# Block-sparse attention and a bilinear FFN on one core: weights loaded after a piece of keys, values scaled per head pair, a third gather place

## The chip, the cores and the metric

One core of a Trainium2 chip runs the whole program. The metric is the device time of one execution in microseconds (us). TensorE (PE, with its weight loads PEld), VectorE (DVE), ScalarE (ACT), GpSimd (POOL) and SyncE (SP) each work through a queue of their own in order; SP, ACT and POOL also issue DMAs.

## The reference

Four batches, eight heads, 768 tokens, head width 64, in blocks of 32 tokens (24 blocks a batch). A query block sees its neighbour blocks, the first, the last and three sampled blocks; the first and last query blocks see all keys.

```python
scores = scale * np.matmul(q, k.transpose(0, 1, 3, 2))
...
scores = np.where(mask, scores, -1000000000.0)
scores = scores - np.max(scores, axis=-1, keepdims=True)
attn = np.exp(scores)
attn = attn / (np.sum(attn, axis=-1, keepdims=True) + 1e-09)
x = np.matmul(attn, v)          # 3072 tokens x 512
out = (x @ w_a) * (x @ w_b) @ w_out   # d_ff 1536
```

The FFN weights come as 64-bit floats; queries, keys and values as 32-bit floats.

## The kernel before

**Units.** A unit is one query block of one batch with its eight heads; 96 units, batch after batch, in chunks of eight (256 tokens). `attend` is a sparse unit, `attend_all` and `attend_quad` the first and last block of a batch. Batch 0 is computed in plain 32-bit floats. Batches 1 to 3 split each scaled operand into a high and a low 16-bit part. When a chunk's eight units are done, `first_products` (L1429) and `second_products` (L1512 to L1514) run its FFN; these matmuls are most of PE's work.

**Order.** No queue is ordered on the chip. `Plan` is a list scheduler that runs while the program is built: each step is a generator that yields what it needs (an `Event`, a place of a `Ring`, or an engine with an estimated time), and the plan emits the step that can begin first, with a rank to break ties. The emitted order is fixed, and each engine's queue then waits in order on the chip. Every estimated time, rank and ring size thus shapes the order of all queues.

**Weights.** `weights(n)` loads 36 pieces of 512 KB (w_a, w_b, w_out of 12 slices) on POOL's queue (L898), the first two right at the start, into six raw places: three fill `stage`, three fill `keysT[1]`. `convert` turns each into 32-bit floats with three DVE operations (L919, L922, L925), bounds it on ACT (L939), and splits it (L946, L947). `weight_scale` sets the scales and multiplies three factors into `f1` in two operations (L958, L961). `stage_freed` fires when the last weights have left `stage`.

**Start.** `keys(0, g)` issues four pieces of batch 0's keys on ACT's queue (L540), `plain_values_in` three pieces of its values there (L590), `plain_queries` its queries on SP's (L878).

**Keys and values of batches 1 to 3.** `keys` and `values` load four head pairs each (`raw_tile`: a ring of `RAW_BUFS = 4` quarters of `stage`). Keys get a scale for each pair. Values: each pair is bounded (L618), then `values_scale` waits for all four bounds, sets one scale for the batch (`set_scale`: an all-reduce on POOL, L440, and three small DVE operations, L443, L446, L449), and only then each pair is split (L629, L630) and stored to the DRAM tensor `vd` on SP's queue (L635).

**Values for a unit.** `gather_after` (SP's queue, L769 to L783) fetches a unit's value blocks into one of `VG_BUFS = 2` places `VG`; a place comes free when the matmuls of the unit two before (`values_into`, L1043) have read it. The starts of the sampled blocks are read into SP's registers for up to four units at a time (L666).

**In a unit.** Scores to PSUM (L975 in batch 0, L984 later), the row maximum (DVE, L1135), its scaling (DVE, L1139 in batch 0, L1141 later), the exponentials (ACT, L1147), the split (L1003, L1006, L1010), a DMA transpose on SP's queue into one of `PT_BUFS = 3` places `pt` (L1187), the values (L1043), and `output`, which divides by the sums (L1348 to L1356).

Of the kernel before, what the change touches and what calls it, by code (L numbers as in the profile page):

```python
# [10 lines left out]
F16 = mybir.dt.float16  # L11
# [36 lines left out]
SM_BUFS = 3  # L48
LATE = 16
AT_ONCE = 4  # L50
NEAR = 8
# [243 lines left out]
def kernel(  # L295
# [55 lines left out]

    stage = kvp.tile([P, RAW_BUFS, 2 * NT * D], F32, name="stage")
    keysT = [kvp.tile([P, H, S], F16, name=f"keysT{i}") for i in range(2)]
    vd = [dram.tile([S, ROW], F16, name=f"vd{b}") for b in range(B)]
# [14 lines left out]
    at_g = at_w + 3 * NF  # L369
    n_at = at_g + NC  # L370
    bound = const.tile([P, n_at], F32, name="bound")
    bound_v = const.tile([P, B * NG], F32, name="bound_v")
    power = const.tile([P, n_at], F32, name="power")
# [14 lines left out]
    eye = const.tile([P, P], F32, name="eye")  # L388
    mark = const.tile([1, 1], F32, name="mark")
    offs = const.tile([1, NB, NR], I32, name="offs")  # L390
    offs_k = const.tile([1, NB, NR], I32, name="offs_k")
# [135 lines left out]
    def raw_tile(b, g, n):  # L527

        yield stage_freed
        t = stage[:, raw_taken[0] % RAW_BUFS]  # L530
        raw_taken[0] += 1
        freed = yield from take("raw", RAW_BUFS)
        return t, freed

    raw_taken = [0]

    def keys(b, g):
        if b == 0:
            t = yield load_way(
                1000, lambda: nc.scalar.dma_start(plain_keys[:, g], k[0, g]), 100000  # L540
            )
            k_ready[0].fire(t)
            return
# [64 lines left out]
    def values(b, g):  # L608

        yield from gate(order[b, 0] - GATE_KV)  # L610
        raw, freed = yield from raw_tile(b, g, 1)
        yield pool_load(1000, lambda: nc.gpsimd.dma_start(raw, v[b, g]))
        if g + 1 < NG:
            plan.start(values(b, g + 1), order[b, 0] - LEAD_V)
        elif b + 1 < B:
            plan.start(keys(b if b == 1 else b + 1, 0), order[b, 0] - LEAD_K)
        t = raw.rearrange("p (t x) -> p t x", t=NT)
        end = yield act(1020, lambda: nc.scalar.activation(  # L618
            junk.rearrange("p f c -> p (f c)")[:, : NT * P].rearrange("p (t x) -> p t x", t=NT),
            t, AF.Abs, accum_out=bound_v[:, b * NG + g : b * NG + g + 1],  # L620
        ))
        v_bound[b].fire(end)
        if g == NG - 1:
            plan.start(values_scale(b), order[b, 0] - LEAD_V)
        yield v_scale[b]
        done = yield from take("ks", KS_BUFS)
        vs = work.tile([P, NT, 2, 2 * D], F16, tag="ks", name=f"vs{b}_{g}", bufs=KS_BUFS)
        s = scale[:, at_v + b : at_v + b + 1]
        yield act(930, lambda: nc.scalar.activation(vs[:, :, 0], t, AF.Copy, scale=s))  # L629
        end = yield dve(1015, lambda: nc.vector.scalar_tensor_tensor(  # L630
            vs[:, :, 1], t, s, vs[:, :, 0], ALU.mult, ALU.subtract
        ))
        freed.fire(end)
        yield SPARE
        end = yield sp(650, 1350, lambda: nc.sync.dma_start(  # L635
            vd[b][:, g * 4 * D : (g + 1) * 4 * D].rearrange("(t p) x -> p t x", p=P),
            vs.rearrange("p t a x -> p t (a x)"),
        ))
        done.fire(end)
        v_stored[b].fire(end)  # L640

    def values_scale(b):
        yield v_bound[b]
        at = at_v + b
        yield dve(150, lambda: nc.vector.reduce_max(
            bound[:, at : at + 1], bound_v[:, b * NG : b * NG + (NG if b else NT // 2)],
            axis=mybir.AxisListType.X,
        ))
        end = yield from set_scale(slice(at, at + 1))
        v_scale[b].fire(end)  # L650
# [31 lines left out]
    def gather_keys(n):  # L682
# [39 lines left out]
        k_free[b].fire(t)  # L722

    def plain_vg(n):
        t = VG[n % VG_BUFS].rearrange("p a x -> p (a x)").bitcast(F32)
        return t.rearrange("p (a x) -> p a x", a=2)
# [27 lines left out]
    def gather_after(n):  # L754
        b, i, x = vg_units[n]
        vg_free[n] = yield from take("vg", VG_BUFS)
        if n + 1 < len(vg_units):
            plan.start(gather_values(n + 1), order[vg_units[n + 1][:2]] - LEAD_G)
        to, of, row = VG[n % VG_BUFS], vd[b], ROW
        if b == 0:  # L760
            to, of, row = plain_vg(n), plain_values, H * D
        dense = i in (0, NB - 1)
        first = vg_holds.get(n % VG_BUFS) != b
        vg_holds[n % VG_BUFS] = None if dense else b

# [118 lines left out]
    def weights(n):  # L884

        f, i = divmod(n, 3)
        if n == 0:
            yield from gate(W_GATE)
        at = n % W_BUFS if n < W_EARLY else W_BUFS // 2 + n % (W_BUFS // 2)
# [210 lines left out]
    def attend(b, i):  # L1100
# [82 lines left out]
        mine = yield from turn("pt", b, i)  # L1183
        kept = yield from take("pt", PT_BUFS)
        mine.fire(0)
        pt = work.tile([P, 8, P], F16, tag="pt", name=f"pt{n}", bufs=PT_BUFS)
        t = yield sp(1300, 1500, lambda: nc.sync.dma_start_transpose(  # L1187
# [5 lines left out]
        yield from before(b, i)  # L1193
        vg = VG[m % VG_BUFS]
        quads = [
# [23 lines left out]
    def attend_quad(b, i, hq, ends):  # L1219
# [52 lines left out]
        for x in range(2):  # L1272
# [13 lines left out]
            freed[x].fire(t)  # L1286
            kept = yield from take("pt", PT_BUFS)
            if x == 1:
                mine_pt.fire(0)
            pt = work.tile([P, 6, P], F16, tag="pt", name=f"pt{n}_{hq}{x}", bufs=PT_BUFS)  # L1290
            t = yield sp(1100, 1130, lambda hl=hl, pt=pt: nc.sync.dma_start_transpose(
# [5 lines left out]
    def all_values(b, i, hq, x, pt, kept):  # L1297
# [17 lines left out]
        else:  # L1315
            vg = VG[m % VG_BUFS].rearrange("p a x -> p (a x)")
            terms = [
# [10 lines left out]

    ride = [Event() for _ in units]
    quad_sent = {(b, i): Event() for b in range(B) for i in (0, NB - 1)}  # L1330
    all_done = {
# [3 lines left out]
    def output(b, i, bank, read):  # L1335
# [288 lines left out]
```

## Time and profile before

| | |
|---|---|
| three timed runs | 803.25, 807.28, 808.39 us, median 807.28 |
| the profiled execution's own time, its span | 803.08 us, 801.3 us |
| busy: PE, DVE, ACT, POOL | 742.4, 533.6, 490.9, 227.6 us |
| mean granted TensorE clock | 0.983 of full speed |
| DMA | 131.8 MB, 164 GB/s over the span |
| the chain of waits by engine | PE 65%, DVE 13%, DMA 9%, issue 5%, ACT 4%, SP's queue 3% |

PE's busy time counts pipelined matmuls whose ends are modelled. The chain of waits is followed back from the last instruction, at each step to what released it. A wait for several semaphores is put down to the one that came last.

### The profile page before, as it was taken

The numbers are of one execution on the slowest core, as the hardware profiler recorded it, in microseconds if no ns is written. First come the engines' busy times: TensorE is split into PE (matmuls) and PEld (weight loads), VectorE is DVE, ScalarE is ACT, GpSimd is POOL, SyncE is SP. The second block draws the span as 40 slices with busy tenths as digits, with TensorE's granted clock in tenths as the row PEclk, the third lists the DMA queues.
The fourth block names the chain that finished last, engine by engine and source line by source line (L and its number), as shares of the span: only waits on it lengthen the run. The fifth ranks groups of instructions, "written<-read, shape, count | busy, mean of one in ns | idle before, by whom it ended". The sixth has DMA issues, their size and how long they took to land.

```text
span 801.3 us, 25888 instructions
## 1 busy us (share of the span) xinstructions
PE 742.4 (93%) x10056; PEld 522.5 (65%) x10056; DVE 533.6 (67%) x1504; ACT 490.9 (61%) x1202; POOL 227.6 (28%) x532
## 2 busy tenths in 40 slices
PE   2759789899998989999999999999989999999997
PEld 0426568674567748757758758658658757768853
DVE  5899999975666677676577686667667775322132
ACT  2666888786656677776466686565566664333333
POOL 5535833212233432202233432302234320000001
PEclk9879999999999999999999999999999999999999
DMA  8776786865577899897579998968687788310001
GB/s 270 234 215 196 228 249 189 266 131 135 126 186 163 182 197 226 179 231 155 144 180 170 214 239 170 210 172 171 155 179 164 147 158 167 91 34 1 2 1 53
DMA packets 184135, 131.80 MB, mean 164 GB/s; under 512 B 135627, under 2 KB 155724, under 8 KB 184012
## 3 DMA queue, kind: packets, MB, share of 16 engines
q1 hardware_dynamic: 170860, 82.89, 50.3%
q0 software_dynamic: 11616, 44.05, 17.5%
q10 hardware_dynamic: 1536, 3.21, 1.3%
q8 instruction: 79, 1.29, 0.7%
q14 instruction: 44, 0.36, 0.2%
HBM read 87.63 MB, written 11.01 MB: 123 GB/s over the span
## 4 chain that ended last, share of the span: by engine, by line
PE 65%; DVE 13%; DMA 9%; issue 5%; ACT 4%; SPq 3%; POOL 0%; POOLq 0%; ACTq 0%; DVEq 0%
PE ab L1429 37%; PE o L1512 6%; PE o L1514 5%; PE o L1513 5%; PE av L1043 5%; PE s L984 4%; DMA VG<-vd 4%; DMA vd<-vs 2%; DMA vp<-in_v_dram 2%; DVE low L1135 1%; SPq L666 1%; DVE wab L947 1%; SPq L783 1%; PE s L1120 1%; PE s L975 1%
## 5 line engine op out<-in xcount | busy, mean ns | idle before, releaser
L1429 PE MATMUL ab<-xT,wab 128*128 128x256 f16 x3456 | 393.2, 273 | 2.8 <-DVE g L1448 2.1
L1429 PEld LDWEIGHTS <-wab 128*128 128x128 f16 x3456 | 332.8, 98 | 58.1 <-issue 16.9
L1448 DVE TENSOR_TENSOR g<-g,ab 128x256 f32<-128x256 f32 x144 | 60.4, 419 | 112.9 <-ACT g L1445 109.3
L1445 ACT ACTIVATE g<-ab,f 128x256 f32<-128x256 f32 x144 | 67.7, 470 | 104.2 <-PE ab L1429 103.2
L1483 DVE SCALAR_TENSOR_TENSOR gh<-g,scale,gh 128x256 f16<-128x256 f32 x144 | 69.5, 494 | 72.0 <-ACT gh L1482 70.9
L1482 ACT ACTIVATE gh<-g,scale 128x256 f16<-128x256 f32 x144 | 70.7, 504 | 74.5 <-PE o L1514 70.6
L1512 PE MATMUL o<-wo,gh 128*128 128x512 f16 x288 | 110.1, 382 | 0.0
L1513 PE MATMUL o<-wo,gh 128*128 128x512 f16 x288 | 109.5, 380 | 0.0
L1514 PE MATMUL o<-wo,gh 128*128 128x512 f16 x288 | 109.5, 380 | 0.0
L710 POOL COPY KG<-keysT 128x128 int32 (+1 forms) x264 | 89.0, 375 | 44.6 <-POOL KG L701 22.5
L701 POOL COPY KG<-keysT 128x384 int32<-128x384 int32 (+1 forms) x86 | 50.6, 589 | 164.6 <-PE s L984 146.0
L1147 ACT ACTIVATE sm<-s,low,cq 128x256 f32<-128x256 f32 x132 | 73.6, 559 | 31.7 <-DVE low L1141 15.6
L440 POOL PARTITION_ALL_REDUCE power<-bound x58 | 25.8, 447 | 180.1 <-DVE bound L1462 103.7
L1043 PE MATMUL av<-VG,pt 128*32 128x128 f16 (+2 forms) x3488 | 63.5, 212 | 13.0 <-DMA VG<-vd 9.4
L1010 DVE SCALAR_TENSOR_TENSOR hl<-sm,hl 128x256 f16<-128x256 f32 (+1 forms) x156 | 69.8, 453 | 1.8 <-ACT hl L1003 0.5
L1135 DVE TENSOR_REDUCE low<-s 128x2 f32<-128x512 f32 x88 | 60.1, 683 | 14.9 <-PE s L984 12.0
L1043 PEld LDWEIGHTS <-pt 128*32 128x32 f16 x2688 | 33.1, 97 | 35.4 <-issue 26.6
L1512 PEld LDWEIGHTS <-gh 128*128 128x128 f16 x288 | 28.2, 98 | 36.9 <-issue 6.0
L1514 PEld LDWEIGHTS <-gh 128*128 128x128 f16 x288 | 28.2, 98 | 34.3 <-issue 0.5
L1513 PEld LDWEIGHTS <-gh 128*128 128x128 f16 x288 | 28.3, 98 | 29.1 <-issue 0.3
L1452 ACT ACTIVATE junk<-g 128x1024 f16<-128x1024 f32 x36 | 38.0, 1055 | 10.4 <-DVE g L1448 10.2
L1006 DVE TENSOR_SCALAR hl<-sm 128x256 f16<-128x256 f32 (+1 forms) x113 | 36.3, 325 | 11.7 <-DMA pt<-hl 8.9
(136 smaller groups left out, 932.3 us busy)
## 6 DMA issues: line engine op xcount, KB each, us to landing
VG<-vd SPq DMA_DIRECT2D x210, 64.0 KB, 3.0
VG<-vd SPq DMA_DIRECT2D x66, 192.0 KB, 3.7
q<-in_q_dram POOLq DMA_DIRECT2D x18, 512.0 KB, 4.9
VG<-vd SPq DMA_DIRECT2D x24, 384.0 KB, 3.7
out_dram<-ou POOLq DMA_DIRECT2D x24, 256.0 KB, 3.6
stage<-in_v_dram POOLq DMA_DIRECT2D x12, 384.0 KB, 4.5
vd<-vs SPq DMA_DIRECT2D x12, 384.0 KB
stage<-in_k_dram POOLq DMA_DIRECT2D x12, 384.0 KB, 6.5
```

The costliest lines, as they stand in the source:

```text
L710: nc.gpsimd.tensor_copy(to[:, :, (5 + r) * w : (6 + r) * w], of[:, :, bass.ds(at, w)])
L1010: t = yield dve(221 + n * 1.03, lambda: nc.vector.scalar_tensor_tensor(lo, sm, over, hi, ALU.mult, ALU.subtract))
L1043: mm(both[hs, :, i % 2, hq] if two else av[hs, i % 2, hq], pt[:, y, hs], of if two or b == 0 else of[:, 0], start=(i % 2 == 0 and hq == 0 ...
L1135: yield dve(685, lambda: nc.vector.tensor_reduce(mx, ps, axis=mybir.AxisListType.X, op=ALU.max, negate=True))
L1147: t = yield act(750, lambda hq=hq: nc.scalar.activation(sm[:, hq], ps[:, hq], AF.Exp, bias=low[:, at, hq, 0:1], scale=factor_of(b, cc, hq) ...
L1429: mm(ab[:, i, :].rearrange("p (j x q) -> p j x q", j=PER // 2, x=2), wab[:, f, i, part, kt, :], xc[:, :, a, :, kt, :], start=(i == 0 and k ...
L1445: yield act(460, lambda: nc.scalar.activation(g, ab[:, 0, :], AF.Copy, scale=f1[:, f : f + 1]))
L1482: yield act(400, lambda: nc.scalar.activation(gh[:, 0], g, AF.Copy, scale=s))
L1483: t = yield dve(480, lambda: nc.vector.scalar_tensor_tensor(gh[:, 1], g, s, gh[:, 0], ALU.mult, ALU.subtract))
L1512: mm(po, gh[:, 0, js], wo[:, f, 0], start=(f == 0), stop=False)
L1513: mm(po, gh[:, 0, js], wo[:, f, 1], start=False, stop=False)
L1514: mm(po, gh[:, 1, js], wo[:, f, 0], start=False, stop=(f == NF - 1))
```

## The change

- The weights' loads start when the second piece of batch 0's keys has landed (`k_early`); a copy of one key element on POOL makes POOL's queue wait for it.
- The scaling of the maxima in batch 0 moves from DVE to ACT.
- `f1` takes one DVE operation in place of two.
- Each head pair of values in batches 1 to 3 gets its own scale, right after its bound. `values_even` then takes the largest of the four, and the ratio of each to it enters the divisor in `output`, with the factor that was there.
- `stage` keeps two raw places for keys and values in place of four. The other half becomes, once the weights have left it, a third gather place for batches 1 to 3 and a fourth place for transposed probabilities.

```diff
+    spare = stage.rearrange("p g x -> p (g x)")[:, RAW_PLACES * 2 * NT * D :]
 def raw_tile(b, g, n):
         yield stage_freed
-        t = stage[:, raw_taken[0] % RAW_BUFS]
+        t = stage[:, raw_taken[0] % RAW_PLACES]
         raw_taken[0] += 1
-        freed = yield from take("raw", RAW_BUFS)
+        freed = yield from take("raw", RAW_PLACES)
 def keys(b, g):
+            if g == 1:
+                k_early.fire(t)
             k_ready[0].fire(t)
 def values(b, g):
-            t, AF.Abs, accum_out=bound_v[:, b * NG + g : b * NG + g + 1],
-        ))
+            t, AF.Abs, accum_out=bound[:, at : at + 1],
+        ))
+        end = yield from set_scale(slice(at, at + 1))
         v_bound[b].fire(end)
         if g == NG - 1:
-            plan.start(values_scale(b), order[b, 0] - LEAD_V)
-        yield v_scale[b]
+            plan.start(values_even(b), order[b, 0] - LEAD_V)
-        s = scale[:, at_v + b : at_v + b + 1]
+        s = scale[:, at : at + 1]
+    def values_even(b):
+        yield v_bound[b]
+        at, to = at_p + (b - 1) * NG, at_v + b
+        yield dve(150, lambda: nc.vector.reduce_max(
+            rscale[:, to : to + 1], rscale[:, at : at + NG], axis=mybir.AxisListType.X
+        ))
+        def factors():
+            for x in range(2):
+                ps = slice(x * D, (x + 1) * D)
+                nc.vector.tensor_scalar(
+                    evened[ps, b], scale[ps, at : at + NG].rearrange("p (a i) -> p a i", i=2)[:, :, x],
+                    rscale[ps, to : to + 1], float(2.0 ** 14), ALU.mult, ALU.mult,
+                )
+        end = yield dve(320, factors)
+        v_scale[b].fire(end)
+    def split_vg(m):
+        at = vg_at[m]
+        if at < VG_BUFS:
+            return VG[at]
+        return spare[:, :ROW].bitcast(F16).rearrange("p (a x) -> p a x", a=2)
+    vg_at = [m % VG_BUFS if m < n_plain else (m - n_plain) % 3 for m in range(len(vg_units))]
+    def take_vg(m):
+        at = vg_at[m]
+        if at >= VG_BUFS:
+            yield stage_freed
+        ev = Event()
+        last = vg_user.get(at)
+        vg_user[at] = ev
+        if last is not None:
+            yield last
+        return ev
 def gather_after(n):
-        vg_free[n] = yield from take("vg", VG_BUFS)
+        vg_free[n] = yield from take_vg(n)
 def weights(n):
         if n == 0:
-            yield from gate(W_GATE)
+            yield k_early
+            yield pool(120, lambda: nc.gpsimd.tensor_copy(mark_w, plain_keys[0:1, 1, 0:1]))
 def weight_scale(f):
-        end = yield dve(160, lambda: nc.vector.tensor_mul(
-            f1[:, f : f + 1], rscale[:, at : at + 1], rscale[:, at + 2 : at + 3]
-        ))
-        end = yield dve(160, lambda: nc.vector.tensor_mul(
-            f1[:, f : f + 1], f1[:, f : f + 1], rscale[:, at + 1 : at + 2]
+        end = yield dve(165, lambda: nc.vector.scalar_tensor_tensor(
+            f1[:, f : f + 1], rscale[:, at : at + 1], rscale[:, at + 1 : at + 2],
+            rscale[:, at + 2 : at + 3], ALU.mult, ALU.mult,
         ))
 def attend(b, i):
         if b == 0:
-            yield dve(165, lambda: nc.vector.tensor_scalar(mx, mx, D ** -0.5, None, ALU.mult))
+            yield act(200, lambda: nc.scalar.mul(mx, mx, D ** -0.5))
...
-        kept = yield from take("pt", PT_BUFS)
+        pt, kept = yield from place_pt(f"{n}", 8)
...
-        vg = VG[m % VG_BUFS]
+        vg = split_vg(m)
+    def place_pt(name, cols):
+        freed = yield from take("pt_split", PT_BUFS + 1)
+        at = pt_taken[0] % (PT_BUFS + 1)
+        pt_taken[0] += 1
+        if at == PT_BUFS:
+            yield stage_freed
+            t = spare[:, ROW : ROW + 4 * P].bitcast(F16).rearrange("p (a x) -> p a x", x=P)
+            return t[:, :cols], freed
+        return work.tile([P, cols, P], F16, tag="pt", name=f"pt{name}", bufs=PT_BUFS), freed
 def output(b, i, bank, read):
-            yield dve(165, lambda: nc.vector.tensor_scalar(
-                dn, dn, EPS, float(2.0 ** 14), ALU.add, ALU.mult
+            yield v_scale[b]
+            yield dve(165, lambda: nc.vector.scalar_tensor_tensor(
+                dn, dn, EPS, evened[:, b].unsqueeze(1).to_broadcast([P, 2, HQ]),
+                ALU.add, ALU.mult,
             ))
```

## Rows read from the trace of the kernel before

**Rows 1.** Stages: window, length, then busy us (count) per engine, clock, DMA, GB/s.
```profile
0.00:12.50 12.50, 0.35 (x4) 0.21 (x4) 3.51 (x22) 1.49 (x2) 3.27 (x8) 1.00 0.86 241
12.50:28.00 15.50, 10.98 (x116) 4.71 (x116) 14.56 (x29) 7.72 (x22) 12.26 (x28) 1.00 0.97 308
28.00:61.00 33.00, 20.24 (x352) 11.67 (x352) 30.08 (x87) 22.52 (x61) 13.76 (x30) 0.73 0.69 208
61.00:125.00 64.00, 55.83 (x906) 39.37 (x908) 62.77 (x157) 50.91 (x138) 37.52 (x73) 0.95 0.74 218
125.00:300.00 175.00, 164.00 (x2246) 112.98 (x2239) 128.77 (x366) 121.40 (x294) 54.65 (x131) 1.00 0.73 175
300.00:700.00 400.00, 394.79 (x5752) 285.78 (x5750) 268.50 (x781) 251.68 (x619) 102.19 (x256) 1.00 0.83 177
700.00:801.30 101.30, 96.16 (x695) 67.76 (x693) 25.44 (x66) 35.22 (x70) 3.98 (x8) 1.00 0.05 18
```

**Rows 2.** PE's waits, 0 to 125 us: total us, times, longest.
```profile
PE av L1380 <- DVE xs L1356: 14.9, 6, 5.2
PE s L1120 <- DVE mrows L516: 8.3, 1, 8.3
PE s L975 <- POOL KG L710: 4.9, 1, 4.9
```

**Rows 3.** PE's waits, 125 to 700 us.
```profile
PE av L1043 <- DMA VG<-vd: 9.4, 8, 2.4
```

**Rows 4.** Timeline of the first 28 us: start, duration, engine, line, idle before.
```profile
2.64 0.68 POOL L898 DMA_DIRECT2D stage<-in_moe_w_a_dram  x1
12.53 0.36 DVE L701 COPY KG<-keysT 128x384 f32<-128x384 f32 x1 [4.27 <-DMA keysT<-in_k_dram]
26.83 1.06 ACT L600 ACTIVATE va<-vp 128x1024 f16<-128x1024 f32 x1 [3.38 <-DMA vp<-in_v_dram]
```

**Rows 5.** DMA queues, 0 to 6 us: packets, MB, share (q10 is ACT's).
```profile
q10 hardware_dynamic: 428, 1.17, 59.5%
```

**Rows 6.** DMA queues, 6 to 10 us (q1 is SP's, q0 POOL's).
```profile
q10 hardware_dynamic: 128, 0.37, 40.4%
q1 hardware_dynamic: 104, 0.35, 37.7%
q0 software_dynamic: 62, 0.25, 26.1%
```

**Rows 7.** Chain of waits, pieces between 75 and 100 us: start, us, what.
```profile
80.32 0.08 DVE low L1139
92.36 0.12 DVE power L443
```

**Rows 8.** Instructions by line: count, ns min/median/max, first and last start.
```profile
L1139 DVE TENSOR_SCALAR low<-low x22: 149/162/1273, 17.7 to 150.4; 128x2 f32<-128x2 f32 x22
L1147 ACT ACTIVATION_READ_ACCUMULATOR sm<-s,low x44: 189/198/218, 18.9 to 153.5; 128x1 f32 x44
L961 DVE TENSOR_TENSOR f<-f,rscale x12: 125/149/239, 44.3 to 164.6; 128x1 f32<-128x1 f32 x12
L440 POOL PARTITION_ALL_REDUCE power<-bound x58: 307/356/1192, 28.3 to 769.5; - x58
```

**Rows 9.** Chain of waits, two pieces between 238 and 245 us.
```profile
238.56 2.50 SPq L666
242.99 2.40 DMA VG<-vd
```

**Rows 10.** SP's queue: its waits, 125 to 700 us.
```profile
SPq L778 <- PE av L1043: 27.7, 19, 6.5
```

**Rows 11.** Timeline: key and value pieces of batch 2, first loads to last stores.
```profile
275.93 1.10 POOL L546 DMA_DIRECT2D stage<-in_k_dram  x2
297.37 1.02 DVE L564 SCALAR_TENSOR_TENSOR ks<-stage,scale,ks 128x768 f16<-128x768 f32 x1
351.91 1.80 SPq L635 DMA_DIRECT2D vd<-vs  x2
```

More of the change, by code (lines that the diff above doesn't have):

```diff
@@ L49 @@
 LATE = 16
+RAW_PLACES = 2
 AT_ONCE = 4
@@ L369 @@
     at_g = at_w + 3 * NF
-    n_at = at_g + NC
+    at_p = at_g + NC
+    n_at = at_p + (B - 1) * NG
     bound = const.tile([P, n_at], F32, name="bound")
-    bound_v = const.tile([P, B * NG], F32, name="bound_v")
+    bound_v = const.tile([P, NT // 2], F32, name="bound_v")
+    evened = const.tile([P, B, HQ], F32, name="evened")
     power = const.tile([P, n_at], F32, name="power")
@@ L389 @@
     mark = const.tile([1, 1], F32, name="mark")
+    mark_w = const.tile([1, 1], F32, name="mark_w")
     offs = const.tile([1, NB, NR], I32, name="offs")
@@ L529, in raw_tile @@
         yield stage_freed
-        t = stage[:, raw_taken[0] % RAW_BUFS]
+        t = stage[:, raw_taken[0] % RAW_PLACES]
         raw_taken[0] += 1
-        freed = yield from take("raw", RAW_BUFS)
+        freed = yield from take("raw", RAW_PLACES)
         return t, freed
     raw_taken = [0]
+    k_early = Event()
     def keys(b, g):
@@ L617, in values @@
         t = raw.rearrange("p (t x) -> p t x", t=NT)
+        at = at_p + (b - 1) * NG + g
         end = yield act(1020, lambda: nc.scalar.activation(
             junk.rearrange("p f c -> p (f c)")[:, : NT * P].rearrange("p (t x) -> p t x", t=NT),
-            t, AF.Abs, accum_out=bound_v[:, b * NG + g : b * NG + g + 1],
+            t, AF.Abs, accum_out=bound[:, at : at + 1],
         ))
+        end = yield from set_scale(slice(at, at + 1))
         v_bound[b].fire(end)
         if g == NG - 1:
-            plan.start(values_scale(b), order[b, 0] - LEAD_V)
-        yield v_scale[b]
+            plan.start(values_even(b), order[b, 0] - LEAD_V)
         done = yield from take("ks", KS_BUFS)
         vs = work.tile([P, NT, 2, 2 * D], F16, tag="ks", name=f"vs{b}_{g}", bufs=KS_BUFS)
-        s = scale[:, at_v + b : at_v + b + 1]
+        s = scale[:, at : at + 1]
         yield act(930, lambda: nc.scalar.activation(vs[:, :, 0], t, AF.Copy, scale=s))
@@ L645, in values_scale @@
         yield dve(150, lambda: nc.vector.reduce_max(
-            bound[:, at : at + 1], bound_v[:, b * NG : b * NG + (NG if b else NT // 2)],
+            bound[:, at : at + 1], bound_v,
             axis=mybir.AxisListType.X,
@@ L722, in gather_keys @@
         k_free[b].fire(t)
+    def split_vg(m):
[3 more added lines that the diff above has]
+        return spare[:, :ROW].bitcast(F16).rearrange("p (a x) -> p a x", a=2)
+    n_plain = sum(u[0] == 0 for u in vg_units)
+    vg_at = [m % VG_BUFS if m < n_plain else (m - n_plain) % 3 for m in range(len(vg_units))]
+    vg_user = {}
+    def take_vg(m):
[8 more added lines that the diff above has]
+        return ev
     def plain_vg(n):
@@ L755, in gather_after @@
         b, i, x = vg_units[n]
-        vg_free[n] = yield from take("vg", VG_BUFS)
+        vg_free[n] = yield from take_vg(n)
         if n + 1 < len(vg_units):
             plan.start(gather_values(n + 1), order[vg_units[n + 1][:2]] - LEAD_G)
-        to, of, row = VG[n % VG_BUFS], vd[b], ROW
         if b == 0:
             to, of, row = plain_vg(n), plain_values, H * D
+        else:
+            to, of, row = split_vg(n), vd[b], ROW
         dense = i in (0, NB - 1)
-        first = vg_holds.get(n % VG_BUFS) != b
-        vg_holds[n % VG_BUFS] = None if dense else b
+        first = vg_holds.get(vg_at[n]) != b
+        vg_holds[vg_at[n]] = None if dense else b
         def copies():
@@ L1183, in attend @@
         mine = yield from turn("pt", b, i)
-        kept = yield from take("pt", PT_BUFS)
+        pt, kept = yield from place_pt(f"{n}", 8)
         mine.fire(0)
-        pt = work.tile([P, 8, P], F16, tag="pt", name=f"pt{n}", bufs=PT_BUFS)
         t = yield sp(1300, 1500, lambda: nc.sync.dma_start_transpose(
@@ L1286, in attend_quad @@
             freed[x].fire(t)
-            kept = yield from take("pt", PT_BUFS)
+            pt, kept = yield from place_pt(f"{n}_{hq}{x}", 6)
             if x == 1:
                 mine_pt.fire(0)
-            pt = work.tile([P, 6, P], F16, tag="pt", name=f"pt{n}_{hq}{x}", bufs=PT_BUFS)
             t = yield sp(1100, 1130, lambda hl=hl, pt=pt: nc.sync.dma_start_transpose(
@@ L1315, in all_values @@
         else:
-            vg = VG[m % VG_BUFS].rearrange("p a x -> p (a x)")
+            vg = split_vg(m).rearrange("p a x -> p (a x)")
             terms = [
@@ L1329 @@
     ride = [Event() for _ in units]
+    pt_taken = [0]
+    def place_pt(name, cols):
[7 more added lines that the diff above has]
+        return work.tile([P, cols, P], F16, tag="pt", name=f"pt{name}", bufs=PT_BUFS), freed
     quad_sent = {(b, i): Event() for b in range(B) for i in (0, NB - 1)}
```

## The prediction

> **What bounds the kernel now.** I read the busy times by stage first [rows 1]. TensorE is busy 394.8 of 400 us from 300 to 700, and 164.0 of 175 from 125 to 300: there it is the bound. Before 125 us it is not: busy 0.35 + 10.98 + 20.24 + 55.83 = 87.4 of 125 us, so 37.6 us idle. After 125 us its idle time is 11.0 + 5.2 + 5.1 = 21.3 us, of which the last 5.1 are the final stores. So a change can gain time only by shortening the 37.6 us, or the 16.2 us between 125 and 700.
>
> Next I read who TensorE waits for. Up to 125 us [rows 2]: 8.3 us for the mask tables, 4.9 us for the first gathered keys, and 14.9 us for the divided sums from VectorE. VectorE itself is busy 30.08 + 62.77 = 92.9 of the 97 us from 28 to 125 [rows 1]; it is the bound of that stretch, and what it is spared there ends the stretch earlier. From 125 to 700 one wait stands out [rows 3]: 9.4 us in 8 places for gathered values. The DMA queues and the SP queue then say why each is late.
>
> **The change, part by part.**
>
> *Weights behind keys.* Batch 0's keys are 8 x 768 x 64 x 4 bytes = 1.57 MB. By 6 us ACT's DMA queue has sent 1.17 MB [rows 5]; of the 0.40 MB left it sends 0.37 in the next 4 us, sharing with queries and the first weights [rows 6]. So the keys are out at about 10.3 us, and VectorE sees them at 12.53 [rows 4]. Without the weights' queue the 0.97 MB of rows 6 are shared by two queues: 0.49 MB each in 4 us, so 0.40 takes 3.3 us, to 9.3: 1.0 us gained. From above it is 4.2 us, since the mask is ready only at 8.3 us [rows 2]. From below it is a loss: half of the keys are out by about 4.7 us (estimate from 1.17 MB at 6 us, the flow beginning near 2.5), seen 2.2 us later as above, so the first weights are issued near 7 in place of 2.64 us [rows 4], a slip of 4.4 us that VectorE pays in full if it has nothing else to do. I take -1.0, near what the queue shares give: VectorE is busy 14.56 of 15.5 us after 12.5 [rows 1], with key copies, maxima and value copies to fill with. Behind the waiting copy POOL's queue holds only weights and key gathers, and the latter need the keys anyhow.
>
> Beside this a rule: the Trainium skill, "DMA: Bandwidth & Descriptors", section "Issuing engines are not separate DMA queues", says that DMAs of all issuing engines run on the same 16 engines and interleave. The trace agrees: three queues share 0.97 MB in 4 us with none idle [rows 6]. By that rule the weights lose what the keys gain; this term would be 0 and the sum -8.0.
>
> *Maxima on ScalarE.* 22 operations leave VectorE [rows 8]. Each lasts 0.162 us, but overlaps the one before it, and the chain shows 0.08 [rows 7]: 22 x 0.08 = -1.8 us, between 0 (if it filled gaps) and -3.6 (full length). What ScalarE pays for a two-element operation no row shows; the nearest is its one-element read of an accumulator, 0.198 us [rows 8]: 0 to 22 x 0.198 = 4.4 us. ScalarE idles 97 - 73.4 = 23.6 us from 28 to 125 [rows 1], which hides it; without that cover it is +4.4.
>
> *One f1 operation less.* 12 of 0.149 us [rows 8], net 0.08: -1.0 us, to -1.8 at full length.
>
> *Scales per head pair.* Twelve all-reduces in place of three, and three small VectorE operations with each. A small one costs 0.08 to 0.12 us [rows 7], so 9 x 3 x 0.1 = 2.7 us for three batches, 0.9 for batch 1; `values_even` has three small operations a batch in place of one maximum, +0.2. Only batch 1 falls in VectorE's stretch or just behind it: +1.1. For batches 2 and 3 VectorE is 67% busy (268.5 of 400 us) [rows 1], which hides it; without that cover +2.2 more. POOL pays 9 x 0.356 = 3.2 us [rows 8]; it is busy 102 of 400 us. Each new all-reduce waits on POOL for its bound from ScalarE, with key gathers queued behind; they are a unit ahead.
>
> *Third gather place.* A gather must wait until the values of the unit two before are used. SP waits for that 27.7 us in 19 places [rows 10], then loses up to 2.50 us to a register load, and the DMA takes 2.40 us [rows 9]; TensorE pays 9.4 us. With three places the gather may go one unit sooner, some 7 us (96 units in about 700 us): more than the register load and the landing together. But SP still issues in one order, and the transposes stand between. I take two thirds, -6.3, between 0 and -9.4. What is late next is the transposes, and ScalarE and VectorE in front of them.
>
> *Fourth transposed place, two raw places.* I cost them at nothing. The first only loosens a ring. The second is hidden by the FFN's stock: after 700 us TensorE still has 96.2 us of work [rows 1], so attention may slip some without TensorE running dry. Without this cover it is the last rival.
>
> Sum: -1.0 - 1.8 - 1.0 + 1.1 - 6.3 = **-9.0 us**. Against the profiled execution's 803.08 us that is 794.1. The four executions shown (803.08, 803.25, 807.28, 808.39) have the middle 805.3, 2.2 above the profiled one, and the timed median is 4.2 above it. I add 2.2: **796 us**.
>
> **The rivals.** A difference under 1% (8.1 us of 807.28) is about what a measurement of this kernel cannot tell from none: under 799.2 is faster, over 815.4 slower.
>
> - *SP's order is the limit, not the place.* The gather gets its place earlier but goes out where the planner puts it, behind transposes and register loads [rows 9]. For it: the 2.50 us register load is not touched. Against: the 27.7 us wait for a place [rows 10]. Then only the start's -2.7 stays: 805.3 - 2.7 = 802.6. Chance 18%.
> - *Values first.* With the weights behind, all three pieces of batch 0's values may be issued at once; the last is seen at 26.83 us now [rows 4], though half of the loads before it were weights. TensorE idles 4.5 us from 12.5 to 28 and 12.8 from 28 to 61 [rows 1]; if a third of these 17.3 us goes, that is -5.8 more: 790. Against: the values' issue waits its turn on ScalarE's queue. Chance 10%.
> - *A new fixed order with new stalls.* Every changed estimate re-orders all queues; a gain of 9.0 us is of the size of the present eight stalls [rows 3]. The places and scales then do what they say, but as much is lost elsewhere: 803 to 808. That the change does not do what it says belongs here: the keys' landing may be early enough already that the wait shifts nothing. Chance 13%.
> - *Slower: two raw places.* A pair of pieces holds its place from the load to the split, 297.37 + 1.02 - 275.93 = 22.5 us [rows 11]. Eight pieces through two places take 4 x 22.5 = 90 us; now the last stores of batch 2 are issued by 353.7, after 77.8 us [rows 11]. So the values of a batch come 12 us later. It decides only if TensorE has no FFN work ready for those 12 us; after 125 us it nearly always has, which speaks against. If two batches go uncovered: 805.3 - 9.0 + 24 = 820. Chance 9%.
>
> **How the numbers follow.** My forecast has 50%, with a range of its own of 788 to 802: the start terms between +1 and -6, the gather term between -3 and -9.4, and 2 for the spread of executions. Of this I put 44 points under 799.2. Faster: 44 + 10 + 4 (the low end of the first rival) = 58%. Within 1%: 6 + 14 + 13 = 33%. Slower: 9%. The range, 785 to 808, takes in the three milder rivals and leaves out the last one and the far ends.
>
> **What would show it.** Keys: the first score matmul at about 12.5 in place of 13.6 us, and the first weights' load issued near 7 us. Maxima and f1: VectorE's busy time down by some 4 us in the first 150 us, ScalarE's up by 2 to 4. Gather: TensorE's wait for gathered values after 125 us falls from 9.4 to about 3 us, SP's wait for a place to a third. Idle before 125 us falls from 37.6 to about 35. My forecast is wrong if the values' wait stays near 9 us, if the maxima's stretch is bound by ScalarE, or if TensorE shows waits for keys or stored values where a batch begins.

## The result, and the profile after

The changed kernel's median is 813.29 us (805.98 to 818.79, 22 executions), that of the kernel before beside it 808.54 (803.00 to 813.51, 22). The ratio is 1.0059 [1.0034, 1.0083]: slower by some 4.8 us, where 796 with a range of 785 to 808 was forecast. Ratios in this text leave out executions that ran over 1.5% above the fastest of their kernel (six of the twelve of e2); medians and ranges do not.

The first profile of the changed kernel was taken in an execution of 818.79 us, the longest of the 22. A second one (e9 below) was of 808.85 us, span 807.1. It stands near the low end of its range, and the 803.08 us of the kernel before at the low end of theirs, so I compare these two and use the first profile only where it shows a wait more plainly. Two profiles of one order can differ: the first one idles 33.3 us before 125 us, like the second, but 40.2 behind it, 5.3 more.

The stage windows of the second profile (columns as in [rows 1]):

```profile
0.00:12.50 12.50, 1.52 (x16) 0.80 (x20) 4.99 (x28) 1.49 (x2) 4.77 (x15) 1.00 0.87 265
12.50:28.00 15.50, 10.66 (x164) 5.75 (x156) 14.00 (x28) 9.31 (x27) 12.11 (x24) 1.00 0.90 282
28.00:61.00 33.00, 23.80 (x394) 13.22 (x388) 32.22 (x84) 22.49 (x66) 14.59 (x30) 0.84 0.72 232
61.00:125.00 64.00, 55.75 (x879) 40.94 (x881) 60.88 (x142) 52.31 (x148) 39.58 (x78) 0.95 0.68 205
125.00:300.00 175.00, 160.40 (x2313) 111.52 (x2302) 132.34 (x386) 123.60 (x305) 56.55 (x139) 1.00 0.77 185
300.00:700.00 400.00, 384.85 (x5579) 280.57 (x5578) 255.35 (x765) 246.79 (x611) 95.06 (x251) 1.00 0.81 174
700.00:807.10 107.10, 101.97 (x744) 70.37 (x742) 27.43 (x70) 37.27 (x74) 4.00 (x8) 0.99 0.05 17
```

TensorE's busy times before 125 us add up to 1.52 + 10.66 + 23.80 + 55.75 = 91.7, so it idles 33.3 us there, 4.3 less than the 37.6 of [rows 1]. Behind 125 us it is busy 647.2 of 682.1 us and idles 34.9, where [rows 1] give 21.3: 13.5 more before rounding. Its busy time over the whole span fell by 3.4 us (742.36 to 738.95). The account closes: -4.3 + 13.5 - 3.4 = +5.8 = 807.1 - 801.3. **The start gained more than forecast, and the long middle, where 6.3 us were to be won, lost twice that.**

Whom TensorE waits for in the second profile, 125 us to the end (total us, times, longest):

```profile
PE ab L1490 <- DVE g L1509: 8.1, 5, 2.8
PE av L1092 <- DMA stage<-hl: 5.2, 4, 1.5
PE av L1092 <- DMA pt<-hl: 4.7, 8, 1.1
PE av L1092 <- ACT pt L1145: 3.1, 3, 1.2
```

The wait for gathered values of [rows 3], 9.4 us, is gone altogether. In its place stand 9.9 us for transposed attention weights (`hl`, into `pt` or into the fourth place in `stage`), and 8.1 us for the gate products `g`, which are ScalarE's and VectorE's work. The first profile shows the same pair from 125 to 700 us:

```profile
PE ab L1490 <- DVE g L1509: 12.3, 4, 5.3
PE av L1092 <- DMA pt<-hl: 6.1, 6, 2.5
PE av L1092 <- DMA stage<-hl: 4.1, 4, 1.3
```

And in the kernel before, over the same stretch, they were small:

```profile
PE ab L1429 <- DVE g L1448: 2.1, 3, 1.8
PE av L1043 <- DMA pt<-hl: 0.5, 1, 0.5
```

The DMA issues say little on why. Kernel before (KB each, median us from issue to landing):

```profile
VG<-vd SPq DMA_DIRECT2D x210, 64.0 KB, 3.0
pt<-hl SPq DMA_TRANSPOSE x90, 3.7
xT<-xo SPq DMA_TRANSPOSE x36, 2.6
```

Changed kernel, second profile:

```profile
VG<-vd SPq DMA_DIRECT2D x147, 64.0 KB, 2.2
pt<-hl SPq DMA_TRANSPOSE x68, 3.6
xT<-xo SPq DMA_TRANSPOSE x36, 3.6
stage<-hl SPq DMA_TRANSPOSE x22, 5.0
```

The gathers land 2.2 us after issue in place of 3.0, the transposes into `pt` alike, those into the fourth place in 5.0. But these medians move as much without the change: that of `xT` is 2.5 to 4.1 in the kernel before and its variants, the gathers' 2.5 to 3.0 there and 2.2 to 3.4 in the changed kernel's orders, and the fourth place's 3.0 to 7.3 in these. A landing is known, too, of few issues (of the 66 sparse units' transposes, 7 in the kernel before and 30 in the second profile). All of these transfers go out through one queue, SP's, whose transfers take 67.9% of the time of the 16 DMA engines from 200 to 700 us; in all profiles that share is 67.0 to 70.6%, so it does not tell the orders apart either.

One place in the timeline of the changed kernel shows how a transpose comes to wait (start, duration, engine, line, idle before):

```profile
262.64 0.42 DVE L1059 SCALAR_TENSOR_TENSOR hl<-sm,hl 128x256 f16<-128x256 f32 x1
265.18 0.52 SPq L828 DMA_DIRECT2D VG<-vd  x1
267.02 1.33 SPq L833 DMA_DIRECT2D VG<-vd  x3
268.45 1.29 SPq L1235 DMA_TRANSPOSE stage<-hl  x1
274.06 0.56 PE L1092 MATMUL av<-VG,stage 128*32 128x128 f16 x30 [0.84 <-DMA stage<-hl]
```

The source of the transpose is complete at 263.06, but SP issues the gather for the same matmuls first (with a load of registers between 265.70 and 267.02). The transpose goes out at 268.45, 5.4 us after its source was ready, and TensorE, which stands for it, goes on at 274.06. This is no new lateness, though. Over the 66 sparse units of batches 1 to 3, with the last split (L1010, now L1059) and the transpose (L1187, now L1235) of each paired in order, a transpose is issued 5.4 us after its source (median) in the kernel before and 5.3 us in the changed kernel. So the runs do not show that the sooner gathers pushed the transposes back; the likelier reading is that the transposes always stood in SP's queue, and that TensorE meets them now that the values no longer hold it up first.

### The profile page after: what moved, and what is told of

It reads as the page before. It is cut to its first block, busy times and chain, and to the rows that moved or that the text cites. A ratio compares the mean times of both kernels' runs of the same rounds, so it can differ in the third digit from the quotient of the medians.

```text
span 817.0 us, 25918 instructions
## 1 busy us (share of the span) xinstructions
PE 743.5 (91%) x10056; PEld 525.1 (64%) x10056; DVE 527.8 (65%) x1497; ACT 492.9 (60%) x1230; POOL 228.2 (28%) x542
## 4 chain that ended last, share of the span: by engine, by line
PE 53%; DVE 16%; DMA 13%; issue 7%; ACT 7%; POOL 2%; SPq 1%; POOLq 1%; ACTq 0%; DVEq 0%
PE ab L1490 34%; DMA pt<-hl 5%; PE av L1092 4%; PE o L1573 4%; PE o L1575 3%; PE o L1574 3%; PE s L1033 3%; DMA keysT<-ks 3%; DMA stage<-hl 3%; DVE low L1184 2%; ACT gh L1543 2%; DVE VG L794 1%; ACT sm L1196 1%; DMA stage<-in_v_dram 1%; DMA stage<-in_moe_w_a_dram 1%
## 5 line engine op out<-in xcount | busy, mean ns | idle before, releaser
L1490 PE MATMUL ab<-xT,wab 128*128 128x256 f16 x3456 | 398.1, 275 | 14.5 <-DVE g L1509 12.8
L738 POOL COPY KG<-keysT 128x128 int32 (+1 forms) x264 | 87.5, 369 | 35.9 <-POOL KG L729 18.4
L1059 DVE SCALAR_TENSOR_TENSOR hl<-sm,hl 128x256 f16<-128x256 f32 (+1 forms) x156 | 71.3, 468 | 2.3 <-ACT hl L1052 1.4
L1092 PE MATMUL av<-VG,pt 128*32 128x64 f32 (+2 forms) x2160 | 40.5, 218 | 9.6 <-DMA pt<-hl 6.1
L1055 DVE TENSOR_SCALAR hl<-sm 128x256 f16<-128x256 f32 (+1 forms) x104 | 31.3, 307 | 17.6 <-DMA pt<-hl 10.8
L1092 PEld LDWEIGHTS <-pt 128*32 128x32 f16 x2032 | 26.0, 98 | 23.4 <-issue 13.3
```

What stands on the lines that cost most here:

```text
L738: nc.gpsimd.tensor_copy(to[:, :, (5 + r) * w : (6 + r) * w], of[:, :, bass.ds(at, w)])
L1059: t = yield dve(221 + n * 1.03, lambda: nc.vector.scalar_tensor_tensor(lo, sm, over, hi, ALU.mult, ALU.subtract))
L1092: mm(both[hs, :, i % 2, hq] if two else av[hs, i % 2, hq], pt[:, y, hs], of if two or b == 0 else of[:, 0], start=(i % 2 == 0 and hq == 0 ...
L1490: mm(ab[:, i, :].rearrange("p (j x q) -> p j x q", j=PER // 2, x=2), wab[:, f, i, part, kt, :], xc[:, :, a, :, kt, :], start=(i == 0 and k ...
```

## The experiments

Two theories stood at the outset. **The raw places** (theory A in the expectations): two places in place of four make the loads of keys and values late, and ScalarE, which waits for them in order, makes the gate products late. **The order**: every queue's order is fixed beforehand from estimates; the changed estimates make a new order, whose stalls cost what the parts gain, and the order of the kernel before is an unusually good one. "Same order" below means that the sequence of instructions on every queue was kept, apart from the edit.

One table first. Idle times are of TensorE, in us, from one profiled execution each, read as above; e9 is the changed kernel itself.

| kernel | median us (range) | ratio to before | idle to 125 | idle after |
|---|---|---|---|---|
| before | 808.5 (803.0 to 813.5) | 1 | 37.6 | 21.3 |
| e5, same order | 805.4 (800.2 to 812.1) | 0.9983 [0.9953, 1.0014] | 39.2 | 21.4 |
| e6, same order | 808.6 (803.8 to 814.5) | 1.0036 [1.0006, 1.0066] | 39.9 | 21.9 |
| e10, same order | 808.5 (805.9 to 812.5) | 1.0027 [1.0001, 1.0054] | 41.9 | 22.4 |
| e16, same order | 804.5 (802.1 to 808.0) | 0.9965 [0.9941, 0.9989] | 39.5 | 23.3 |
| e7, before, new order | 832.9 (821.6 to 839.8) | 1.0195 [1.0141, 1.0249] | 41.0 | 41.7 |
| e8, before, new order | 808.1 (802.1 to 816.2) | 1.0015 [0.9980, 1.0050] | 40.2 | 24.6 |
| e11, before, new order | 825.0 (819.1 to 836.4) | 1.0216 [1.0176, 1.0256] | 37.8 | 32.6 |
| e14, before, new order | 811.5 (803.9 to 818.6) | 1.0034 [0.9990, 1.0078] | 40.4 | 22.5 |
| after (e9's profile) | 813.3 (806.0 to 818.8) | 1.0059 [1.0034, 1.0083] | 33.3 | 34.9 |
| e4, after, new order | 819.3 (818.0 to 824.5) | 1.0139 [1.0100, 1.0178] | 36.3 | 36.0 |
| e13, after, new order | 815.0 (803.9 to 820.1) | 1.0128 [1.0082, 1.0174] | 35.9 | 29.9 |
| e12, after, new order | 817.3 (809.8 to 821.1) | 1.0103 [1.0050, 1.0156] | 36.7 | 32.4 |
| e15, after, new order | 817.1 (813.1 to 819.5) | 1.0116 [1.0075, 1.0157] | 34.5 | 38.9 |
| e1, after less places | 813.4 (806.8 to 820.1) | 1.0076 [1.0041, 1.0111] | 33.3 | 30.5 |
| e2, after less places | 815.3 (803.6 to 823.6) | 1.0020 [0.9981, 1.0060] | 34.3 | 28.5 |
| e3, after, slack | 822.5 (820.5 to 826.1) | 1.0175 [1.0137, 1.0214] | 34.6 | 38.4 |

**e1 and e2: are the places to blame?** e1 takes the third gather place and the fourth transposed place away and has four raw places again; e2 takes away the same two but keeps two raw places.

```diff
-RAW_PLACES = 2                                  (e1 only)
+RAW_PLACES = 4
-    vg_at = [m % VG_BUFS if m < n_plain else (m - n_plain) % 3 ...]
+    vg_at = [m % VG_BUFS for m in range(len(vg_units))]
-        freed = yield from take("pt_split", PT_BUFS + 1)
+        freed = yield from take("pt_split", PT_BUFS)
```

> The changed kernel with four raw places, two gather places and three transposed places again; the weights' wait, the two small edits and the scales per head pair stay. Theory A (two raw places make keys and values late, and ScalarE and POOL stand behind late loads): TensorE's wait for the gate product (ab behind g) after 125 us falls from 12.3 us to under 4, its wait for gathered values comes back to 6 to 10 us, and the time is 803 to 808 us, under the changed kernel's 813. Theory B (any new order brings its own stalls): 808 to 816 us, with other waits.

> The changed kernel with two raw places kept, but without the third gather place and the fourth transposed place. Theory A: TensorE pays both the late loads (8 to 14 us of waits for the gate product or for keys) and the gathered values (6 to 10 us): 815 to 824 us, at least 8 us above the same kernel with four raw places. Theory B: the two differ by under 4 us.

By the medians neither comes back to the kernel before; by its ratio e2 does, within the interval. Two raw places do not cost the 8 us of theory A: by the ratios the kernel with two is not the slower one (1.0020 against 1.0076, intervals that overlap), by the medians it is 1.9 us slower. ScalarE waits 11.5 us for pieces of values after 125 us in e1, with four raw places, and 14.6 and 7.8 in the changed kernel's two profiles, with two; and e2, with two, has the shortest wait for the gate product of the changed kernel's orders, 1.5 us. The raw places are not the cause. What TensorE waits for in e1 from 125 us on is telling:

```profile
PE av L1092 <- DMA VG<-vd: 8.4, 9, 1.6
PE ab L1490 <- DVE g L1509: 4.4, 4, 2.0
PE av L1092 <- DMA pt<-hl: 3.0, 3, 1.3
```

Without the third place the wait for values is back, 8.4 us, and the transposes fall from 9.9 to 3.0: the two places exchange the one for the other at no gain in time (1.0076 without them, 1.0059 with them).

The other profiles agree. In the seven with both places (the changed kernel's two, e3, e4, e12, e13, e15) TensorE waits 0 to 3.0 us for gathered values and 7.6 to 10.3 for transposes between 125 and 700 us. In the nine without them (the kernel before, e1, e2, e5 to e8, e11, e14) it is 7.6 to 12.0 and 0.4 to 4.9. The two waits together come to 9.0 to 12.9 us and to 8.9 to 15.6. **So this exchange comes with the two places, in every order that was planned for them.** The wait for the gate product does not part the two groups so: 4.5 to 12.3 us in the seven, 0.8 to 7.8 in the nine. (e10 and e16, below, have a third place for 16 units only and stand in neither group.)

**e3: time for the loads.** The planner is told to let 4 us pass between a load's landing and its use by ScalarE.

```diff
+        yield 4000        (behind the load, in keys() and in values())
```

> The changed kernel, with 4 us more in the planner's estimate of when a key or value piece of batches 1 to 3 has landed; no instruction is added. Theory A, in the form that the late landings catch ScalarE's queue because the order is laid out for a landing that is too early: TensorE's wait for the gate product after 125 us falls from 12.3 us to under 4, ScalarE's waits for loads into the stage from 14.6 us to under 5, and the time is 803 to 808 us. Theory B: 808 to 816 us, the waits only change their place.

It became slower, 1.0175, although what theory A blames went away. ScalarE no longer waits for a load into the stage after 125 us (14.6 us in the first profile of the changed kernel, 7.8 in the second), and TensorE's wait for the gate product is 5.3 us (12.3 and 8.1); yet TensorE idles 38.4 us. The late loads were real: in the first profile of the changed kernel ScalarE stood 6.07 us for a value piece whose load went out 9 us before, and the gate product behind it cost TensorE 5.30 us.

```profile
502.83 0.54 POOL L620 DMA_DIRECT2D stage<-in_v_dram  x1 [3.60 <-ACT g L1506]
512.22 0.84 ACT L627 ACTIVATE junk<-stage 128x768 f16<-128x768 f32 x1 [6.07 <-DMA stage<-in_v_dram]
516.49 1.86 PE L1490 MATMUL ab<-xT,wab 128*128 128x256 f16 x8 [5.30 <-DVE g L1509]
```

Taking them away did not help, but an estimate that re-orders everything cannot tell what they cost. So the next runs keep either the edit or the order fixed.

**e4 and e7: the same kernels, one estimate altered.** The planner's allowance for the landing of gathered values goes from 2500 to 2600 ns, in the changed kernel (e4) and in the one before (e7). Nothing else changes, but all queues are planned anew.

```diff
-LATE_VG = 2500
+LATE_VG = 2600
```

> The changed kernel with one estimate of the planner altered by 100 ns (a gather's lateness 2600 in place of 2500); no instruction is added, only the order of the queues may differ. Theory A: the waits of the changed kernel stay, and the time is within 3 us of its 813. Theory B: the time moves by more than 4 us, either way, and the waits sit in other places.

> The kernel before with one estimate of the planner altered by 100 ns (a gather's lateness 2600 in place of 2500): no instruction is added or taken, only places in the queues change. Theory B (a new order by itself costs, because the order of the kernel before happens to be a good one): 4 to 12 us over the kernel before. If the change's own parts cost the time, this stays within 2 us of it.

The changed kernel (e4) moves by 6 us, to 819.3, with other waits (values 1.9, transposes 9.8, gate products 5.6), as theory B has it. The kernel before (e7) becomes 2% slower without any of the change, more than theory B foretold. In e7's profile TensorE waits for transposes too, but the values stay late:

```profile
PE av L1043 <- DMA VG<-vd: 12.0, 11, 2.0
PE s L984 <- ACT sm L1147: 6.5, 1, 6.5
PE av L1043 <- ACT pt L1096: 5.1, 3, 2.2
PE av L1043 <- DMA pt<-hl: 3.6, 3, 2.0
```

**e8 and e13, e11 and e12, e14 and e15: three more estimates**, each altered alike in the kernel before (first of the pair) and in the changed one.

```diff
-LATE_PT = 2500      (e8, e13)
+LATE_PT = 2600
-LANDING = 1200      (e11, e12)
+LANDING = 1250
-M_ACT = 50          (e14, e15)
+M_ACT = 40
```

> The kernel before with another estimate altered by 100 ns (a transpose's lateness 2600 in place of 2500). Theory B: 3 to 12 us over the kernel before. If the change's own parts cost the time: within 2 us of it.

> The kernel before with the planner's landing estimate at 1250 in place of 1200 ns; only the order differs. Theory B: over the kernel before by 2 to 15 us. If the change's own parts cost the time: within 2 us.

> The changed kernel with the same altered landing estimate, 1250 ns. Theory B: somewhere between 805 and 825 us, and on average no worse than the kernel before under the same kind of alteration. If the change's own parts cost the time: 813 to 820 us, clearly over the kernel before with this estimate.

> The changed kernel with the transpose's lateness estimate at 2600 in place of 2500 ns, the partner of e8. Theory B (the order of the kernel before is an unusually good one; the change's parts are worth little): 808 to 822 us. Theory E (the change's own parts cost time): over its partner, 808.1, by 5 us or more, as in each other pair.

> The kernel before with the planner's safety margin of ScalarE at 40 in place of 50 ns; only the order differs. Theory B: 810 to 830 us. Theory E: within 3 us of the kernel before.

> The changed kernel with the same margin, 40 ns, the partner of e14. Theory B: 808 to 825 us, not over its partner by more than 5 us. Theory E: over its partner by 5 us or more.

Of the altered orders of the kernel before, e11 (17.4 us over it by the ratio) lies above theory B's range and e8 (1.2) below it; e14 (2.7) fits both theories. The changed kernel stands over its partner by 5 us or more in e13 and e15, as theory E has it, and under it in e12 and e4.

With the unaltered pair these are five. By the ratios, changed kernel minus kernel before under the same estimates is +0.59, -0.56 (e4, e7), +1.13 (e13, e8), -1.13 (e12, e11) and +0.82% (e15, e14). Their mean is +0.17%, or +1.4 us, with a 95% interval of 1.2% on either side (their standard deviation is 0.97, over the root of five, times 2.8): from -8 to +11 us. By the medians the mean is -0.14%. So **what the change is worth apart from the order is not settled; it is near nothing, and a few us either way are open**. The order is worth more than that: by estimates alone the kernel before goes from 1 to 1.0216, the changed kernel from 1.0059 to 1.0139. In e11 the waits for gate products and transposes grow without the change, beside that for values:

```profile
PE ab L1429 <- DVE g L1448: 7.8, 6, 4.2
PE av L1043 <- DMA VG<-vd: 7.6, 6, 2.4
PE av L1043 <- DMA pt<-hl: 4.9, 4, 2.3
```

**e5, e6 and e10: parts of the change under the old order.** e5 puts POOL's copy of a key element in front of the first weights' load. e6 scales the maxima on ScalarE and fuses the `f1` operations, while the planner goes on with its old durations. e10 gives 16 units of batch 1 a third gather place, in a part of the key buffer that is free by then; it issues two more block fetches.

```diff
 (e5)
+            if n == 0:
+                nc.gpsimd.tensor_copy(mark_w, plain_keys[0:1, 1, 0:1])
             nc.gpsimd.dma_start(raw, (w_a, w_b, w_out)[i][f].bitcast(I32))
 (e6)
-            yield dve(165, lambda: nc.vector.tensor_scalar(mx, mx, D ** -0.5, None, ALU.mult))
+            yield dve(165, lambda: nc.scalar.mul(mx, mx, D ** -0.5))
 (e10)
+        if m0 <= m < m0 + 16:
+            return (2, (m0 + 1) % 2, m0 % 2)[(m - m0) % 3]
+        return m % VG_BUFS
```

> The kernel before, every queue in its old order; only the copy of a key element stands in POOL's queue ahead of the first weights' load, so that the load waits for the second piece of keys. Theory C (the wait itself is worth what the first term of the sum says, and what the changed kernel loses comes from its new order): first score matmul at about 12 in place of 13.6 us, time 1 to 4 us under the kernel before. Theory D (the weights come too late for VectorE): VectorE idles more before 28 us and the time is 2 to 5 us over.

> The kernel before, every queue in its old order, with the two small edits alone: the 22 scalings of maxima go from VectorE to ScalarE at the same places of the order, and f1 takes one operation. Theory C: VectorE is spared some 3 us before 150 us, time 1 to 4 us under the kernel before. Against it: ScalarE's 22 operations of 0.2 us stand in front of exponentials and gate copies, and TensorE waits more for them: 0 to 3 us over.

> The kernel before, every queue in its old order, with a third gather place for 16 units of batch 1 alone (order 25 to 40); the place lies in the other batch's keys, which are unused then, and two block fetches are added. Theory C (a third place by itself takes away the wait for gathered values): the waits for gathered values between 200 and 300 us, 5.5 us in 3 places before, fall to under 2, and the time is 2 to 5 us under the kernel before. Against it: in the old order SP still issues the gather where it stood, behind transposes, so 4 us or more of the wait stay or go over to the transposes, and the time is within 2 us.

In us, by the ratios: e5 -1.4 [-3.8, +1.1], e6 +2.9 [+0.5, +5.3], e10 +2.2 [+0.1, +4.4]. None gives a gain that can be measured, and e6 and e10 cost a little. In e5 the first score matmul starts at 12.72 us in place of 13.56, and VectorE is busy 17.8 us before 28 us, 18.1 in the kernel before, so theory D did not come true. The scales per head pair and the two raw places were not tried under the old order. In e10 SP no longer waits for a place from 200 to 300 us (3.8 us in 5 places in the kernel before), and yet TensorE waits there for values 6.5 us in 4 places (5.5 in 3 before; under 2 by theory C). One place, SP's and TensorE's timeline of e10:

```profile
222.87 0.44 PE L1058 MATMUL av<-VG,pt 128*32 128x128 f16 x24
231.60 0.56 SPq L792 DMA_DIRECT2D VG<-vd  x1
233.29 1.33 SPq L797 DMA_DIRECT2D VG<-vd  x3
236.06 1.95 SPq L1383 DMA_TRANSPOSE xT<-xo  x1
238.07 0.57 SPq L792 DMA_DIRECT2D keysT<-vd  x1
238.09 0.67 PE L1058 MATMUL av<-VG,pt 128*32 128x128 f16 x24 [2.40 <-DMA VG<-vd]
```

TensorE stands 2.40 us for the gather that SP issued from 231.60 to 234.62. With three places in turn, its place was last read no later than 223.31: it had been free for 8 us, and its turn in SP's queue had not come. The next gather, into the third place (`keysT`), goes out at 238.07, behind two transposes.

**e16: e5 and e10 together**, again in the old order.

> The kernel before in its old order with both the weights' wait of e5 and the third gather place for 16 units of e10. If the two were independent gains they would add: e5 stood 1.5 us under the kernel before, e10 2.3 us over, so 804 to 810 us; nothing clear is expected under 800.

804.48 us, ratio 0.9965 [0.9941, 0.9989]: the one kernel of all that beats both, by 2.8 us [0.9, 4.8]. Its two edits alone measured -1.4 and +2.2, and TensorE still waits 10.0 us for values in it, so which of them gains stays open. One interval of 95% that leaves out 1 on the fast side, among sixteen kernels, may also be chance.

**e9: the changed kernel once more**, for the second profile.

> The changed kernel once more, unaltered, for a second profile of the same order: both theories expect 806 to 818 us. If the waits of the first profile belong to the order, TensorE waits again 8 us or more for the gate product after 125 us, near 484 and 511; if they are luck of a DMA, that wait falls under 5 us and the time under 813.

Neither holds in full. TensorE waits 8.1 us for the gate product, but only 3.3 of them near 484 and 511, where the first profile has 8.9; and the time is 808.85 us. The wait belongs to the order, its size at those two places in part to the execution.

## Why the prediction was wrong

**The failed step is the gather term**, -6.3, and with it the sentence "What is late next is the transposes", which named the next wait and gave it no price beyond the third that the term leaves out. The wait for values did fall, further than forecast (about 3 expected, 0 measured). But the transposes took 9.9 us where they had 0.5, and by the sixteen profiles above that exchange comes with the places: the term was worth nothing. Gate products took 8.1 where they had 2.1; the idle time behind 125 us rose by 13.5. The prediction looked at one row of SP's waits for a place and not at what else stands in its queue. Three readings would have warned:

- Of the 27.7 us of [rows 10], only 15.6 in 15 places lie from 200 us on, where the late values are; the rest is batch 0's. In the changed kernel it is still 14.8 in 12 places: a sooner place lets the planner put the gather sooner in SP's queue, until it waits for its place again.
- [rows 10] show one of the two large rows. With the other (L769, the gathers for a batch's first and last block) SP waited 64.8 us for places from 125 to 700 us in the kernel before; in the changed kernel it is 65.7, where a fall to a third was forecast. That other row, and the two of the changed kernel's second profile:

```profile
SPq L769 <- PE av L1043: 37.1, 15, 6.4
SPq L828 <- PE av L1092: 36.6, 16, 13.0
SPq L819 <- PE av L1092: 29.1, 14, 5.9
```
- In the kernel before a transpose already stood 5.4 us (median) in SP's queue after its source was ready. A transfer that stands so close behind the values is the next wait, and it could be read from the trace.

**The rival "a new fixed order with new stalls" is the best account of the rest**, at 13% and priced 803 to 808; which stall comes from which estimate no run shows. Its size was wrong: [rows 3] were taken as the size of an order's stalls, but they are those of a good order. Five kernels with that order idle 21.3 to 23.3 us after 125 us, whichever edit they carry; other orders of the two kernels idle 22.5 to 41.7. Four altered estimates made the kernel before slower by 0.15, 0.34, 1.95 and 2.16%, the first two within their intervals, and none faster: any edit that changes a planned duration draws from that spread, and the kernel before stands near its good end, as far as four draws can tell.

**"SP's order is the limit, not the place"** (18%, 802.6) is right where the order stays: e10. "Slower: two raw places" (9%, 820) had the sign; e1, e2 and e3 speak against its mechanism.

**The start terms were right in sign and small.** The first score matmul came at 11.33 us (12.01 in the first profile; 12.5 forecast), the first weights were issued at 5.47 (7 forecast, 2.64 before). VectorE's first copy of keys came at 10.30, 2.2 us sooner, where the term had 1.0. Changed kernel, second profile:

```profile
5.47 0.68 POOL L949 DMA_DIRECT2D stage<-in_moe_w_a_dram  x1
10.30 0.36 DVE L729 COPY KG<-keysT 128x384 f32<-128x384 f32 x1 [2.35 <-DMA keysT<-in_k_dram]
11.33 1.94 PE L1024 MATMUL s<-KG,QZ 128*32 128x256 f32 x16 [2.98 <-POOL KG L738]
16.74 1.06 ACT L608 ACTIVATE va<-vp 128x1024 f16<-128x1024 f32 x1 [1.06 <-DMA vp<-in_v_dram]
```

What the rival "values first" (10%) names came true besides: the last piece of batch 0's values is taken at 16.74 us, not at 26.83 [rows 4], and TensorE's idle time from 28 to 61 us falls from 12.8 to 9.2. Idle before 125 us is 33.3 to 36.7 in all nine profiles of the changed kernel and its variants, 37.6 to 41.9 in all nine of the kernel before and its variants, no overlap: means of 34.7 and 39.7, a gain of 5.0 where 2.7 were forecast. e5 and e6 do not show it in the old order (in e5 the last piece of values is still taken at 25.27), so it needs the new one; the earlier values are the likeliest reason, which no run here shows by itself.

The waits that shifted in this stretch, second profile, 0 to 125 us:

```profile
PE tp L1140 <- ACT sm L1196: 11.6, 9, 3.3
PE av L1441 <- DVE xs L1417: 6.0, 4, 3.1
PE s L1024 <- POOL KG L738: 3.0, 1, 3.0
```

And one row of the kernel before, over the same stretch:

```profile
PE tp L1091 <- ACT sm L1147: 7.4, 7, 1.8
```

The wait for VectorE's sums fell from 14.9 [rows 2] to 6.0, and ScalarE's exponentials are next: 11.6, where they were 7.4, 4.2 more against the 8.9 that VectorE gave back.

**Maxima, f1 and scales** went where they were put. ScalarE's scaling was bounded at 0 to 0.198 us an operation and lasts 0.203; the all-reduces are 67 in place of 58:

```profile
L1188 ACT ACTIVATE low<-low x22: 187/203/223, 15.5 to 158.3; 128x2 f32<-128x2 f32 x22
L445 POOL PARTITION_ALL_REDUCE power<-bound x67: 308/354/872, 19.5 to 775.4; - x67
```

In the first 150 us VectorE is busy 132.6 us, 2.6 less than before (4 forecast), ScalarE 106.2, 2.8 more (2 to 4 forecast). Under the old order the -1.8 and -1.0 for maxima and `f1` gave no gain: e6 is +2.9 us [+0.5, +5.3].

## What to carry to other kernels

Where one engine issues both the transfers you want earlier and those that are next in line, read what stands in its queue before you price a freed place, and how long: a place without a free turn gains nothing (e10), and the wait can pass on to the next transfer in line, here from 9.4 us for values to 9.9 for transposes. Where the order of all queues is planned from estimates, measure the spread between orders first, by small changes of an estimate alone; an effect smaller than that spread has to be tested with the order held fixed. A kernel whose order happens to be a good one can look better than an edit of it that plans anew.

## What the runs showed of the hardware

Executions of one and the same kernel differ by 10 us and more, and part of that goes with the granted clock of TensorE. The kernel before was timed beside the runs in four groups of 17 to 29 executions. In each of them the executions with the lower mean clock tend to be the longer ones: the correlation is -0.41 to -0.73, and 0.01 of full speed goes with 2.9 to 6.8 us. In the group with the strongest (23 executions, beside e1) the mean clock lies between 0.970 and 0.985 and the time between 800.9 and 815.3 us. The changed kernel's orders ran at about the same clock (means of 0.977 to 0.983, the kernel before 0.978 to 0.980), so the clock does not explain the result. Which of the two is cause, idle time or clock, the runs do not tell.
